# Fifteen of 37 zeroing transfers issued in attention turns 33 to 37, six routing steps a turn from the start, W1's split one half a turn

## The chip, the cores and the metric

The kernel runs on one core of one Trainium2 chip. The metric is device time in microseconds (us): the median of three runs of the kernel before is 985.14 us (985.03 to 985.75). Engines are named as in the profile: PE is TensorE (PEld its weight loads), DVE VectorE, ACT ScalarE, POOL GpSimd. SP issues DMA transfers; "SPq" is its queue of issues.

## The reference: what is computed

Local attention over chunks of 64 positions, then a mixture of 8 experts of which each token takes two.

```python
def _attn_ref(q, k, v):                 # (8, 8, 576, 64) each
    scores = scale * matmul(q_c, k_c^T)         # per chunk of 64
    attn = exp(scores - max); attn /= sum + 1e-9
    return matmul(attn, v_c)
...
def _moe_ref(x, w_gate, w_noise, noise, w1, w2):   # x: (4608, 512)
    noisy_logits = x @ w_gate + log1p(exp(x @ w_noise)) * noise
    top2 = the two largest of 8; top2_w = softmax over them
    for e in range(8):                  # w1[e]: 512x1024, w2[e]: 1024x512
        h = maximum(x[mask] @ w1[e], 0)
        out[mask] += top2_w[mask, k] * (h @ w2[e])
```

## The kernel before, in words

**Attention in turns.** The 4608 tokens are 36 tiles of 128. `attend(it)` is one turn of a software pipeline: it does the scores of tile it+1, the softmax of tile it, the product with V of tile it-2 (`pv`), the transpose of tile it-3 (`x_trans`, `x_copy`) and, every fourth turn, the gate. Turns 0 to 35 run in a loop; 36 and 37 stand between the first transposes of the expert part, and 38 to 40 are called from inside the first expert block. The program sets the order on each engine by hand (`manual_schedule`): an engine's queue holds its instructions in the order in which the Python code emits them. SP loads Q, K and V in pairs of tiles into rings of three.

**Routing.** `route(g)` is a generator that computes, for a group of four tiles (the last group has eight), the two experts of each token and a slot number in a DRAM list (`lii`). It gives control back before each DVE instruction or pair ("a step"), and a turn takes STEPS steps of it, half before and half after the normalisation (`rc`, `xs`). STEPS is 10 up to turn 13 and 6 after it. When a group is routed, its eight scatters go into `pending`.

**Scatters.** `scatter` (L606 to L623) emits on POOL one or two small memsets (L619), a copy that reads an operand of this turn, so that the scatter keeps its place (L621), and an indirect DMA that writes 128 token rows to `slots` in DRAM (L623). There are 72: group 3 is complete with the 32nd, group 6 with the 56th, the last group with the 72nd. The 32nd is followed by SP's loads of the rows of block 0, the 56th by those of block 1, the last by those of block 2 (`gather`, L170); each of these loads waits until the scatters before it have landed.

**Zeroing.** Results are added to `out` by indirect DMA, so all 37 pieces of 128 rows of `out` are first written with zeros (`zero_out`, L691 to L694, 256 KB each, issued by SP). They are emitted after `layer1` of block 0, which puts them on SP's queue behind the row loads of block 1 and ahead of those of block 2.

**W1's split.** The matmuls are float32r in three terms, so each weight is split into a high part (ACT, L88) and a low part (L89). For expert 0's W1 (four chunks `c`, two halves each) the low part is computed on POOL; the eight halves are emitted two a turn in turns 8 to 11.

**Experts.** Each expert has about 1200 rows in three blocks of about 384. `layer1(i)` does 96 matmuls of 384 columns (L236), `layer2(i)` products of 512 columns (L236 too). While `layer2(1)` runs, its hook transposes the rows of block 2 on PE (`x_tile`, L219) at four fixed places; the first is after the sixth step of row tile 0. All of SP's later loads follow in its queue.

Of the kernel before, what the change touches and what calls it, by code (L numbers as in the profile page):

```python
# [49 lines left out]
def kernel(ctx, tc, qT, kT, vh, wgn, noise, w1, w2, out, caps=CAPS):  # L50
    nc = tc.nc
# [15 lines left out]
    def w_load(e, which, c):  # L67
        st = stage.tile([P, 1024], FT, name="st")
        staged[e, which, c] = st
        if which == 1:  # L70
            if e == 0:
                nc.sync.dma_start(st, w1[0, c * P:(c + 1) * P, :])
            else:
                for j in range(4):
                    nc.sync.dma_start(st[32 * j:32 * j + 32], w1v[ds(place[e], 1), c, j].rearrange("o r f -> (o r) f"))
        else:
            nc.sync.dma_start(st.rearrange("p (f n) -> p f n", f=2),
                              w2[ds(place[e], 1) if e else slice(0, 1), 2 * c * P:(2 * c + 2) * P, :]
                              .rearrange("o (f p) n -> p (o f) n", f=2))

    def w_split(e, which, c, half, eng=None):
        if half == 0:
            W[e, which, c] = (wpool[which].tile([P, 1024], FR, name=f"w{which}h{c}"),
                              wpool[which].tile([P, 1024], FR, name=f"w{which}l{c}"))
        hi, lo = W[e, which, c]
        st = staged[e, which, c]
        s = slice(half * 512, half * 512 + 512)
        nc.scalar.activation(hi[:, s], st[:, s], AF.Copy)  # L88
        (eng or nc.vector).tensor_sub(lo[:, s], st[:, s], hi[:, s].bitcast(FT))  # L89
# [243 lines left out]
    def load_qk(j):  # L333
        if j < NT // 2:
            QB[j] = loads.tile([P, 2, 4, P], FT, name="qb", bufs=RING)
            for h in range(2):
                nc.sync.dma_start(QB[j][h::2], qT[HALF[h], 2 * j:2 * j + 2])
                nc.sync.dma_start(KB[j % RING][h::2, h], kT[HALF[h], 2 * j:2 * j + 2])

    def load_v(j):  # L340
        if j < NT // 2:
            for h in range(2):
                nc.sync.dma_start(VB[j % RING][h::2, h], vh[HALF[h], 2 * j:2 * j + 2])
# [76 lines left out]
    def scores(t):  # L420
        for hp in range(4):
            for q in HALF:
                nc.tensor.matmul(PS[q, t % 2, hp * P:(hp + 1) * P], QB[t // 2][:, t % 2, hp, q],  # L423
                                 KB[t // 2 % RING][:, :, t % 2, hp, q], start=True, stop=True)

    def soft_max(t):
        mx = work.tile([P, 4, 2], FT, name="mx", bufs=6)
        nc.vector.tensor_reduce(mx, sco[t % 2], AX.X, OP.max)  # L428
        return mx

    def soft_sub(t, mx):
        PR[t] = work.tile([P, 512], FT, name="pr")
        nc.vector.tensor_tensor(by_head(PR[t]), sco[t % 2], mx[:, :, :, None].to_broadcast([P, 4, 2, 64]), OP.subtract)  # L433

    def soft_exp(t):
        nc.scalar.activation(PR[t], PR[t], AF.Exp, scale=0.125)

    def p_trans(t):
        for hp in range(4):
            nc.tensor.transpose(PS[:, 2, hp * P:(hp + 1) * P], PR[t][:, hp * P:(hp + 1) * P], ident)  # L440

    def p_copy(t):
        PT[t] = work.tile([P, 4, P], FT, name="pts", bufs=2)
        nc.scalar.activation(PT[t].rearrange("p a b -> p (a b)"), PS[:, 2, :], AF.Copy)
# [3 lines left out]
    def pv(t):  # L448
        for hp in range(4):
            for c, q in enumerate(HALF):  # L450
                o = 130 * (hp % 2)
                nc.tensor.matmul(PS[q, 3 + hp // 2, o:o + 130], PT[t][:, hp, q],  # L452
                                 VB[t // 2 % RING][:, :, t % 2, c, hp, :], start=True, stop=True)

    def norm_a(t):
        RC[t] = work.tile([P, 2, 4, 1], FT, name="rc", bufs=6)
        nc.scalar.activation(RC[t], pvb[:, :, :, 64:65], AF.Identity, bias=eps)

    def norm_b(t):
        nc.vector.reciprocal(RC[t], RC[t])  # L460
# [4 lines left out]
    def x_trans(t):  # L465
        x = XS[t // 4][:, t % 4]
        for d in range(ND):
            nc.tensor.transpose(PS[:, 5, d * P:(d + 1) * P], x[:, d * P:(d + 1) * P], ident)  # L468

    def x_copy(t):  # L470
        g, r = divmod(t, 4)
        if r == 0:
            XT[g] = gx.tile([P, ND, 4, P], FT, name="xt", bufs=1)
        nc.scalar.activation(XT[g][:, :, r, :], PS[:, 5, :].rearrange("p (d n) -> p d n", d=ND), AF.Copy)
# [3 lines left out]
    def gate_mm(g):  # L478
        for d in range(ND):
            nc.tensor.matmul(PS[32 * d:32 * d + 32, 6, :], wg[:, d, :], XT[g][:, d], start=True, stop=True)  # L480
# [7 lines left out]
    def gate_turn(g):  # L488
        for r in range(4):
            nc.tensor.transpose(PS[:, 6, r * P:(r + 1) * P], LS[g][:, r, :], ident)  # L490
# [170 lines left out]
    def step_route(phase, most=99):  # L661
        for r in list(routing):
            while r[1] == phase and most > 0:
                if phase == "dve":
                    most -= 1
                r[1] = next(r[0], None)
            if r[1] is None:
                routing.remove(r)

    def next_turn():  # L670
        for r in routing:
            if r[1] == "wait":
                r[1] = next(r[0])
# [13 lines left out]
    wq = list(halves)  # L687
    zeros = list(range(NROWS // P))

    def zero_out(n):  # L690
        for _ in range(n):  # L691
            if zeros:
                r = zeros.pop(0)
                nc.sync.dma_start(out[r * P:(r + 1) * P, :], zero[:, 0:DM])  # L694

    def attend(it):
        STEPS = 6 if it > 13 else 10
        if it % 2:
            load_qk((it - 1) // 2 + 3)
        if it % 2 == 0 and it >= 4:  # L700
            load_v((it - 4) // 2 + 3)
        if it in (9, 11):
            for r in range(CLEAN + 64 * (it // 2 - 4), CLEAN + 64 * (it // 2 - 3), 16):
                nc.sync.dma_start(slots[r * NE:(r + 16) * NE, 0:USED], zero)
        if it == 11:
            nc.sync.dma_start(slots[(CLEAN + P) * NE:NLIST * P * NE, CODE:USED].rearrange("(p r) c -> p r c", p=P),
                              zero[:, 0:3 * (NLIST * P - CLEAN - P) // 16].rearrange("p (r c) -> p r c", c=3))
        if it in range(4, 8):
            w_load(0, 1, it - 4)
        if it in (29, 31, 33, 35):  # L710
            w_load(0, 2, (it - 29) // 2)
        next_turn()
        if it == 0:
            scores(0)
        if it <= 1:
            p_trans(0) if it else scores(1)
        if 0 < it < NT - 1:
            scores(it + 1)
        if 0 <= it - 2 < NT:
            pv(it - 2)  # L720
        gated = it - 4 >= 0 and (it - 4) % 4 == 3
        if gated:
            gate_mm((it - 4) // 4)
        if 0 < it - 1 < NT:
            p_trans(it - 1)
        if 0 <= it - 3 < NT:
            x_trans(it - 3)
        if it - 5 >= 0 and (it - 5) % 4 == 3:
            gate_turn((it - 5) // 4)
            if grp_of[it - 5] != grp_of.get(it - 4):  # L730
                r = route(grp_of[it - 5])
                routing.append([r, next(r)])
        step_route("pe")
        if 0 <= it - 2 < NT:
            norm_a(it - 2)
        if 0 <= it - 1 < NT:
            p_copy(it - 1)
        if it < NT:
            mx = soft_max(it)
            soft_sub(it, mx)  # L740
            scatter(1, mx[0:1, 0, 0:1])
            soft_exp(it)
        if 0 <= it - 3 < NT:
            x_copy(it - 3)
        if gated:
            gate_copy((it - 4) // 4)
        step_route("dve", STEPS // 2)
        if 0 <= it - 2 < NT:
            norm_b(it - 2)
            scatter(1, RC[it - 2][0:1, 0, 0])  # L750
            norm_c(it - 2)
        if it - 5 >= 0 and (it - 5) % 4 == 3:
            gate_sum((it - 5) // 4)
        step_route("act")
        step_route("dve", STEPS // 2)
        if it == NT + 2:
            scatter(2, XT[(it - 3) // 4][0:1, 0, (it - 3) % 4, 0:1])
        elif it == NT + 3:
            scatter(2, LS[(it - 4) // 4][0:1, 0, 0:1])
        if it in range(8, 12):  # L760
            for _ in range(2):
                w_split(0, 1, *wq.pop(0), eng=nc.gpsimd)

    for it in range(NT):
        attend(it)
# [16 lines left out]
    rot["tr"] = 1  # L782
    x_tile(0, 0)
    attend(NT)
    x_tile(0, 1)
    x_tile(0, 2)
# [220 lines left out]
```

## Time and profile before

| | |
|---|---|
| median of three runs | 985.14 us |
| the profiled execution: time, span | 983.39 us, 981.6 us |
| PE, DVE, ACT, POOL busy | 97%, 47%, 29%, 24% |
| turns 0 to 35 (attention) | 0 to about 131 us |
| block 0, block 1, the rest of the experts | from 137 us, from 175 us, from 206 us |
| DMA moved | 132.93 MB, 135 GB/s on average |

A row of a timeline gives start, duration, engine, line, operation and operands, and in brackets how long the engine stood idle before and what ended that. A row of the windows gives, for one stretch, the busy time of each engine with its instruction count, the granted TensorE clock (1.00 is 2.4 GHz, 0.50 is 1.2 GHz) and the busy share of the 16 DMA engines. A stretch whose clock stands between the two held some of each.

### The profile page before, as it was taken

How to read it: one execution, taken by the hardware profiler on the slowest of the kernel's cores; microseconds unless marked ns; L12 is line 12 of the kernel's file. 1: busy time of each engine (PE TensorE's matmuls, PEld its weight loads, DVE VectorE, ACT ScalarE, POOL GpSimd, SP SyncE). 2: the span in 40 equal slices, each digit the busy share in tenths (PEclk: the TensorE clock that was granted, in tenths of full speed). 3: DMA queues.
4: the chain of work that ended last, by engine and by line, in shares of the span. 5: the costliest groups of instructions: out<-in, count | busy, mean ns of one | idle time of the engine just before them, and what ended most of it. 6: DMA issues, size and time to landing. Idle time of an engine off the chain costs nothing.

```text
span 981.6 us, 16116 instructions
## 1 busy us (share of the span) xinstructions
PE 949.9 (97%) x5752; PEld 845.1 (86%) x5752; DVE 459.5 (47%) x1014; ACT 287.8 (29%) x623; POOL 234.8 (24%) x424
## 2 busy tenths in 40 slices
PE   6999999969999999999999999999999999999996
PEld 5778888949897998989898899889998998899885
DVE  6888966214454642554254435443434344434311
ACT  3666662103142421332142213122312231223100
POOL 3366668430201011111101110210111011111112
PEclk9999999979999999999999999999999999999999
DMA  8999965997702643165227522653174216412213
GB/s 303 361 340 374 348 238 213 382 235 137 182 25 48 173 111 44 33 154 140 35 37 149 141 44 33 138 145 54 22 161 129 52 25 161 108 14 30 33 22 44
DMA packets 97155, 132.93 MB, mean 135 GB/s; under 512 B 23440, under 2 KB 56592, under 8 KB 97072
## 3 DMA queue, kind: packets, MB, share of 16 engines
q1 hardware_dynamic: 80160, 92.50, 31.1%
q0 software_dynamic: 16432, 38.33, 19.6%
q8 instruction: 46, 0.75, 0.3%
q10 hardware_dynamic: 480, 1.05, 0.3%
q14 instruction: 37, 0.30, 0.1%
HBM read 81.69 MB, written 50.13 MB: 134 GB/s over the span
## 4 chain that ended last, share of the span: by engine, by line
PE 88%; SPq 4%; DVE 3%; issue 1%; DMA 1%; POOL 1%; ACT 1%; ACTq 0%; DVEq 0%; POOLq 0%
PE PS L236 77%; SPq L694 3%; PE PS L423 3%; PE PS L452 3%; PE PS L440 2%; PE PS L468 1%; PE PS L288 1%; PE PS L480 1%; DVE xs L463 1%; POOL out L203 0%; DMA kb<-in_kT 0%; DMA xg<-slots 0%; DVE mx L428 0%; DVE pr L433 0%; PE PS L490 0%
## 5 line engine op out<-in xcount | busy, mean ns | idle before, releaser
L203 POOL DMA_INDIRECT out<-o,lid x74 | 115.0, 1554 | 646.2 <-DVE o L271 627.0
L236 PE MATMUL PS<-xh,w1h 128*128 128x384 f32 (+2 forms) x768 | 261.3, 340 | 0.0
L236 PE MATMUL PS<-xh,w1l 128*128 128x384 f32 (+2 forms) x768 | 260.5, 339 | 0.0
L236 PE MATMUL PS<-xl,w1h 128*128 128x384 f32 (+2 forms) x768 | 260.4, 339 | 0.0
L255 ACT ACTIVATE hh<-PS 128x384 fp32r<-128x384 f32 (+2 forms) x192 | 95.2, 496 | 463.0 <-PE PS L236 456.9
L236 PE MATMUL PS<-w2h,hh 128*128 128x512 f32 x584 | 228.8, 392 | 0.0
L236 PE MATMUL PS<-w2h,hl 128*128 128x512 f32 x584 | 228.4, 391 | 0.0
L236 PE MATMUL PS<-w2l,hh 128*128 128x512 f32 x584 | 228.3, 391 | 0.0
L258 DVE SCALAR_TENSOR_TENSOR hl<-PS,hh 128x384 fp32r<-128x384 f32 (+2 forms) x192 | 108.7, 566 | 176.1 <-ACT hh L255 144.1
L271 DVE TENSOR_SCALAR o<-PS,lwt 128x512 f32<-128x512 f32 (+2 forms) x74 | 55.4, 749 | 229.5 <-PE PS L236 223.0
L236 PEld LDWEIGHTS PS<-xh,w1h 128*128 128x128 f32 x768 | 144.3, 188 | 5.9 <-issue 4.2
L236 PEld LDWEIGHTS PS<-xl,w1h 128*128 128x128 f32 x768 | 144.3, 188 | 1.6
L236 PEld LDWEIGHTS PS<-xh,w1l 128*128 128x128 f32 x768 | 144.2, 188 | 0.9
L236 PEld LDWEIGHTS PS<-w2h,hl 128*128 128x128 f32 x584 | 109.5, 188 | 23.4
L236 PEld LDWEIGHTS PS<-w2h,hh 128*128 128x128 f32 x584 | 109.7, 188 | 22.6
L236 PEld LDWEIGHTS PS<-w2l,hh 128*128 128x128 f32 x584 | 109.7, 188 | 22.6
L623 POOL DMA_INDIRECT slots<-xs,lii x72 | 71.2, 989 | 26.3 <-issue 23.5
L226 ACT ACTIVATE xh<-y 128x512 fp32r<-128x512 f32 x67 | 41.2, 614 | 92.4 <-DVE y L223 92.4
L227 DVE TENSOR_TENSOR xl<-y,xh 128x512 fp32r<-128x512 f32 x67 | 45.0, 671 | 47.9 <-ACT xh L226 47.9
L423 PE MATMUL PS<-kb,qb 128*64 128x128 f32 x576 | 42.0, 292 | 8.4 <-DMA kb<-in_kT 6.6
L202 POOL MEMSET spacer<- 1x1 f32 x77 | 47.3, 614 | 0.0
L223 DVE STREAM_TRANSPOSE y<-xg 128x512 f32<-128x512 f32 x67 | 45.6, 680 | 0.0
(128 smaller groups left out, 692.3 us busy)
## 6 DMA issues: line engine op xcount, KB each, us to landing
st<-in_w SPq DMA_DIRECT2D x36, 512.0 KB, 6.7
xg<-slots SPq DMA_DIRECT2D x252, 64.0 KB, 2.0
st<-in_w SPq DMA_DIRECT2D x112, 128.0 KB, 4.1
out<-zero SPq DMA_DIRECT2D x37, 256.0 KB, 4.4
vb<-in_vh SPq DMA_DIRECT2D x36, 260.0 KB, 5.2
qb<-in_qT SPq DMA_DIRECT2D x34, 256.0 KB, 5.7
kb<-in_kT SPq DMA_DIRECT2D x32, 256.0 KB, 5.5
xg<-slots SPq DMA_DIRECT2D x9, 256.0 KB, 3.0
```

Of the source, the lines that this page charges most:

```text
L202: nc.gpsimd.memset(spacer, 0.0)
L203: s = nc.gpsimd.indirect_dma_start(out=out, out_offset=bass.IndirectOffsetOnAxis(ap=rows_of(i, j)[0:r], axis=0), in_=o[0:r], in_offset=Non ...
L223: nc.vector.transpose(y[:, 0:4 * r], x[:, 0:4 * r])
L226: nc.scalar.activation(oh, src, AF.Copy)
L227: nc.vector.tensor_sub(ol, src, oh.bitcast(FT))
L236: nc.tensor.matmul(p, a, b, start=first and n == 0, stop=last and n == 2)
L255: nc.scalar.activation(hh[:, 0:n], p, AF.Relu)
L258: nc.vector.scalar_tensor_tensor(hl[:, 0:n], p, 0.0, hh[:, 0:n].bitcast(FT), op0=OP.max, op1=OP.subtract)
L271: nc.vector.tensor_scalar(o[0:r], p[0:r], w, None, op0=OP.mult)
L423: nc.tensor.matmul(PS[q, t % 2, hp * P:(hp + 1) * P], QB[t // 2][:, t % 2, hp, q], KB[t // 2 % RING][:, :, t % 2, hp, q], start=True, stop ...
L452: nc.tensor.matmul(PS[q, 3 + hp // 2, o:o + 130], PT[t][:, hp, q], VB[t // 2 % RING][:, :, t % 2, c, hp, :], start=True, stop=True)
L623: s = nc.gpsimd.indirect_dma_start(out=slots, out_offset=bass.IndirectOffsetOnAxis(ap=lii[:, k, t0 + r:t0 + r + 1], axis=0), in_=XS[(t0 + ...
```

## The change

`STEPS` is 6 in all turns. In each of turns 33 to 37 `zero_out(3)` stands behind the second half of the routing steps, so that 15 of the 37 pieces are emitted there; the call after `layer1` of block 0 stays and emits the 22 that are left. The eight halves of expert 0's W1 are emitted one a turn in turns 7 to 14.

```diff
     def attend(it):
-        STEPS = 6 if it > 13 else 10
+        STEPS = 6
...
         step_route("act")
         step_route("dve", STEPS // 2)
+        if it in range(33, 38):
+            zero_out(3)
...
-        if it in range(8, 12):
-            for _ in range(2):
-                w_split(0, 1, *wq.pop(0), eng=nc.gpsimd)
+        if it in range(7, 15):
+            w_split(0, 1, *wq.pop(0), eng=nc.gpsimd)
```

On SP, from turn 32 on: the last V load (`vb`), the last two loads of W2 (`st`), the rows of block 1 (`xg`, `meta`) and, at the end, those of block 2 (three tiles and one of 64 rows).

```order
 L343 DMA vb_113<-in_vh 64x1040 x2
-L77 DMA st<-in_w 128x2x512 x2
+L77 DMA st<-in_w 128x2x512
+L694 DMA out<-zero 128x512 x6
+L77 DMA st<-in_w 128x2x512
+L694 DMA out<-zero 128x512 x9
 L170 DMA xg<-slots 128x512 x3
 L638 DMA meta_89<-slots 128x3x3
-L694 DMA out<-zero 128x512 x37
+L694 DMA out<-zero 128x512 x22
 L170 DMA xg<-slots 128x512 x3
 L170 DMA xg<-slots 64x512
```

Fifteen zeroing transfers moved ahead of block 1's rows; the V load stands ahead of all of them, one W2 load behind six.

On POOL, before, the low parts of W1 (two halves to a row) and the first scatter, whose copy reads `mx` of turn 13:

```order
L89 TENSOR_TENSOR w1l_529<-st,w1h_528 128x512 x2
L89 TENSOR_TENSOR w1l_597<-st,w1h_596 128x512 x2
L89 TENSOR_TENSOR w1l_649<-st,w1h_648 128x512 x2
L89 TENSOR_TENSOR w1l_715<-st,w1h_714 128x512 x2
L619 MEMSET spacer 1x1 x2
L621 COPY spacer<-mx 1x1
L623 DMA slots<-xs,lii 44032x576
```

The same place now; the first scatter's copy reads `rc` of turn 14:

```order
L89 TENSOR_TENSOR w1l_478<-st,w1h_477 128x512 x2
L89 TENSOR_TENSOR w1l_589<-st,w1h_588 128x512 x2
L89 TENSOR_TENSOR w1l_702<-st,w1h_701 128x512 x2
L89 TENSOR_TENSOR w1l_815<-st,w1h_814 128x512
L619 MEMSET spacer 1x1 x2
L621 COPY spacer<-rc 1x1
L623 DMA slots<-xs,lii 44032x576
L89 TENSOR_TENSOR w1l_815<-st,w1h_814 128x512
L619 MEMSET spacer 1x1 x2
L621 COPY spacer<-mx 1x1
L623 DMA slots<-xs,lii 44032x576
```

The first scatter stands three places of the turns later (turn 14's second instead of turn 13's first), and one half of W1 stands behind it.

On DVE, before, turn 9 and the start of turn 10, from the first routing step of group 0 on:

```order
L521 SCALAR_TENSOR_TENSOR gu<-gu,gy 128x32
L523 TENSOR_TENSOR gsp<-gsp,gu 128x32
L525 SCALAR_TENSOR_TENSOR gsp<-lg,gsp 128x32
L527 TENSOR_TENSOR gsp<-gsp,nz 128x32
L529 TENSOR_TENSOR gsp<-gsp,lg 128x32
L460 RECIPROCAL rc<-rc 128x8
L463 TENSOR_TENSOR xs<-PS,rc 128x512
L535 MAX gm<-gsp 128x8 x4
L539 MAX_INDEX gmi<-gm,gsp 128x8 x4
L543 TENSOR_TENSOR goh<-e_row,gmi 128x32
L428 TENSOR_REDUCE mx<-PS 128x8
```

The same place now:

```order
L521 SCALAR_TENSOR_TENSOR gu<-gu,gy 128x32
L523 TENSOR_TENSOR gsp<-gsp,gu 128x32
L525 SCALAR_TENSOR_TENSOR gsp<-lg,gsp 128x32
L460 RECIPROCAL rc<-rc 128x8
L463 TENSOR_TENSOR xs<-PS,rc 128x512
L527 TENSOR_TENSOR gsp<-gsp,nz 128x32
L529 TENSOR_TENSOR gsp<-gsp,lg 128x32
L535 MAX gm<-gsp 128x8 x2
L428 TENSOR_REDUCE mx<-PS 128x8
```

Two instructions fewer stand ahead of `rc` and `xs`, and the maxima and indices spread into the next turn.

## Rows read from the trace of the kernel before

**Rows 1.** The page: the chain that ended last, shares by engine

```profile
PE 88%; SPq 4%; DVE 3%; issue 1%; DMA 1%; POOL 1%; ACT 1%; ACTq 0%; DVEq 0%; POOLq 0%
```

**Rows 2.** PE's waits, first 225 us: total us, times, longest

```profile
PE PS L219 <- DMA xg<-slots: 9.5, 1, 9.5
```

**Rows 3.** The chain that ended last, 155 to 215 us: start, us, what

```profile
160.96 2.75 DMA slots<-xs,lii
...
191.67 0.65 SPq L694
...
201.93 4.27 DMA xg<-slots
206.25 1.12 PE PS L219 x4
207.37 4.03 PE PS L236 x12
211.83 2.76 PE PS L236 x12
```

**Rows 4.** Timeline of SP's issues, 123 to 202 us

```profile
123.90 1.21 SPq L343 DMA_DIRECT2D vb<-in_vh  x2
...
163.73 1.34 SPq L170 DMA_DIRECT2D xg<-slots  x3
...
165.73 36.09 SPq L694 DMA_DIRECT2D out<-zero  x37
```

**Rows 5.** The first 22 zeroing issues (L694): duration ns min/median/max, start us

```profile
L694 SPq DMA_DIRECT2D out<-zero x22: 481/1252/1667, 165.7 to 191.1; - x22
```

**Rows 6.** Row loads of block 2 (L170, 200 to 206 us): issue to landing

```profile
DMA to landing us min/median/max: 4.4/4.4/4.4
```

**Rows 7.** Timeline of PE: two places of it

```profile
131.48 1.11 PE L452 MATMUL PS<-vb,pts 128*64 128x130 f32 x16
...
167.56 0.60 PE L219 MATMUL PS<-ident,xg 128*128 128x128 f32 x4
```

**Rows 8.** Windows of all engines; the first row names the columns

```profile
core 0: us, PE busy (x) PEld busy (x) DVE busy (x) ACT busy (x) POOL busy (x), PEclk, DMA share, GB/s
35.30:64.57 29.27, 25.42 (x311) 20.61 (x310) 25.27 (x85) 18.85 (x46) 16.01 (x27) 0.94 0.98 338
67.94:91.26 23.32, 23.31 (x307) 19.16 (x306) 20.31 (x78) 14.79 (x38) 16.07 (x49) 1.00 0.99 367
42.50:46.00 3.50, 3.06 (x24) 2.66 (x24) 3.34 (x10) 2.49 (x6) 0.38 (x2) 0.53 1.04 378
...
137.00:157.00 20.00, 19.29 (x128) 17.89 (x126) 14.16 (x74) 9.87 (x23) 15.08 (x34) 1.00 0.39 150
...
200.00:204.00 4.00, 0.00 (x0) 0.00 (x0) 0.00 (x0) 0.00 (x0) 0.00 (x0) 0.50 1.01 352
```

**Rows 9.** Scatters (L623), 155 to 185 us: duration ns, start us; issue to landing

```profile
L623 POOL DMA_INDIRECT slots<-xs,lii x21: 956/982/998, 154.4 to 183.0; - x21
...
DMA to landing us min/median/max: 2.7/6.4/8.0
```

**Rows 10.** The V load of 123.9 us (L343): issue to landing

```profile
DMA to landing us min/median/max: 6.1/6.1/6.1
```

**Rows 11.** Timeline of POOL: a pair of halves, scatters 1, 2 and 32

```profile
37.65 2.50 POOL L89 TENSOR_TENSOR w1l<-st,w1h 128x512 fp32r<-128x512 f32 x2 [28.60 <-ACT w1h L88]
...
56.75 1.18 POOL L623 DMA_INDIRECT slots<-xs,lii  x1 [1.49 <-DMA kb<-in_kT]
...
58.88 1.00 POOL L623 DMA_INDIRECT slots<-xs,lii  x1 [0.47 <-issue]
...
117.81 0.98 POOL L623 DMA_INDIRECT slots<-xs,lii  x1 [0.44 <-issue]
```

**Rows 12.** Timeline of DVE: the same product in group 0 and in group 1

```profile
37.76 1.21 DVE L527 TENSOR_TENSOR gsp<-gsp,nz 128x32 f32<-128x32 f32 x1
...
56.25 0.19 DVE L527 TENSOR_TENSOR gsp<-gsp,nz 128x32 f32<-128x32 f32 x1
```

## The prediction, made before the changed kernel ran

> **What bounds the kernel now.** I read the chain that ended last first: PE carries 88% of it and SP's queue 4% [rows 1]. The rest is read where the chain leaves PE. Of PE's waits in the first 225 us one stands out: 9.5 us of the transposes of L219 for a row load [rows 2]. The chain in order of time says why [rows 3]: the 56th scatter (160.96 us) lets SP load block 1's rows at 163.73, then SP issues 37 zeroing transfers in 36.09 us [rows 4], and only behind them, at 201.93, stand block 2's rows. They land 4.3 us later, and PE, idle since 206.25 - 9.5 = 196.75, goes on at 206.25. It goes on slowly: in the idle stretch the granted clock had fallen to 0.50, the lower level of 1.2 GHz [rows 8], and the four transposes take 1.12 us where the same four took 0.60 at full clock [rows 7], twelve matmuls 4.03 us where the next twelve take 2.76 [rows 3]. The stall thus costs 9.5 + 0.52 + 1.27 = 11.3 us. Behind it PE runs without gaps for most of 750 us, so that what is saved here reaches the end.
>
> A second place is the start of routing. Turns 9 to 15 take 29.27 us and turns 17 to 23, with as many gate turns, 23.32 [rows 8]: 5.95 us more, part of it waits, part a stretch at 0.53 of the clock.
>
> **Part 1: 22 instead of 37 transfers ahead of block 2's rows.** The first 22 start between 165.7 and 191.1 us [rows 5], and the next stands at 191.67 [rows 3]. Block 2's rows are then issued at 191.67 instead of 201.93, 10.26 us earlier. With the 4.4 us that they took to land behind a full queue of the same transfers [rows 6] they are there at 196.07. PE wants them at 196.75: a margin of 0.68 us. The wait goes, the clock does not fall, the sum is -11.3 us. What is late next is near: the last of the 72 scatters, which these loads wait for, and whose kind takes 6.4 us to land in this stretch, 8.0 at most [rows 9]. It is issued at 183.0 [rows 9], so it lands between 189.4 and 191, just ahead of the issue. Bounds of this part: -11.3, and, with a remaining wait of 4 us (below), -5.5.
>
> **Part 2: fifteen transfers in turns 33 to 37.** In the order they stand on SP behind the last V load (123.90 us) and ahead of block 1's rows, which SP cannot issue before 163.73 [rows 4]. Between these SP has some 37 us in which it only waits. Fifteen issues at 0.98 us (36.09 / 37) to 1.25 us [rows 5] are 15 to 19 us, and end near 145. One load of W2 stands behind six of them, so about 7 us later; its halves are split in the last quarter of block 0's first layer, after 150 us. The data are 15 x 256 KB = 3.9 MB, at the 378 GB/s of the windows when the engines are full [rows 8] 10.4 us of all DMA engines. From 137 to 157 us these are busy 0.39 of the time [rows 8], which leaves 12 us. So I cost this part at nothing; its cover is that idle DMA time, and without it it is the slow rival below.
>
> **Part 3: six steps and one half a turn.** In turns 8 to 11 ACT and POOL now split one half, not two, and DVE takes two instructions fewer ahead of `rc` and `xs` in turn 9. The turns from 9 on can gain between 0 and 5.95 us. I expect most of it at that place, and almost none of it at the end, because scatters set the pace: POOL issues them one behind the other, the second at 58.88 and the 32nd at 117.81 [rows 11]. The 32nd releases SP, whose V load for the last two tiles is issued at 123.90 and 124.5 and lands 6.1 us later [rows 4, 10], at 130.6. PE takes that V at 131.48 [rows 7]. PE can thus come at most 0.9 us earlier here, however early the turns before it are, unless the scatters are earlier too.
>
> Are they? The first started at 56.75 after waiting 1.49 us for a DMA, not for its turn [rows 11]. In the changed order it stands three places later, in turn 14, but turn 14 comes earlier by what the turns gain, so I take it at the same time. Behind it POOL now has one half of W1, 2.50 / 2 = 1.25 us [rows 11]. The chain of scatters is later by 1.25 us at the most, and earlier by 0.25 if the 1.49 us go; later turn waits inside the chain shrink when turns are early. I take +0.7.
>
> PE then waits before that V product, for up to 5.95 - 0.9 = 5 us, and the clock may fall. The trace has two prices for it: about 3.5 x 0.47 = 1.6 us in the stretch from 42.5 to 46 us, after a short wait [rows 8], 1.8 after the long one. Since PE is not the bound of turns 36 to 38 I take half, 0.9. Part 3: -0.9 + 0.7 + 0.9 = +0.7 us, between -1.2 and +2.2. It moves block 1's rows and PE alike, so part 1 keeps its margin.
>
> The shared-port rule of the Trainium skill ("SBUF — State Buffer", "SBUF: two separate sides") speaks against this part: a DVE operation with two SBUF inputs and a GpSimd operation that reads SBUF lock each other out for a whole instruction. The same DVE product takes 1.21 us while POOL splits W1 and 0.19 when it does not [rows 12], which agrees. What it would cost is a rival.
>
> **Sum.** -11.3 + 0.7 = -10.6 us. The profiled execution took 983.39 us with a span of 981.6, the median is 985.14, 1.75 above; against its own time the changed kernel should take 972.8 in a profile and, by the median, 974.5 us.
>
> **Rivals.**
>
> Block 2's rows are still late (20%). If all 22 issues keep the median of 1.25 us, they end at 165.73 + 22 x 1.25 = 193.2; if SP then also waits for the last scatter, or the rows need the 6 to 8 us that scatters took, they land at 198 to 201, and PE waits 2 to 4 us, with up to 1.8 us of clock. The gain is 10.6 minus 2 to 5.8, the time 976.5 to 980.3. For it speaks that the margin is 0.68 us; against it that the first 22 did end at 191.67 in this trace.
>
> The low halves on POOL hold DVE up (10%). Each of eight halves in its own turn could hold DVE for 1.21 - 0.19 = 1.0 us; in the trace pairs of halves do this in four turns. Eight such holds, of which the turns before had some four, are 4 us more. If they delay the first scatter, everything behind it is later by that: 978.5. Against it: a product that comes after the half has ended pays nothing.
>
> The early turns' gain arrives (8%). Were the V load no limit, because the scatters start 3 to 5 us earlier, the end would gain as much more: 970 to 971.5. Against it: the 1.49 us wait on a DMA at the first scatter, and the half behind it.
>
> The zeroing comes out of the scatters' time (9%). If the moved 10.4 us of DMA work are not hidden in 126 to 157 us but delay the 56th scatter by all of that, block 1's rows are issued at 174 instead of 163.73. PE wants them at 167.56 [rows 7], 3.8 us after that issue, about what a landing takes, so it waits 10 us and restarts at the low clock, 1.8 us; and 22 issues at 1.25 us from 176 on end at 203.5, block 2's rows land at 208, when PE, 11.8 us late, wants them. The end is later by 11.8 - 11.3 = 0.5 us and, if those rows too take 6 to 8 us, by 2 to 4: about 988. It decides from about 9 us of delay. Against it: beside 22 zeroing transfers scatters land in 2.7 to 8.0 us [rows 9], which is 5 us from best to worst, and not 10.
>
> The Trainium skill speaks to this in "DMA: Bandwidth & Descriptors", "Queues, rings and completion order": each DMA engine takes turns between the queues that have work; by it zeroing would halve the scatters' rate while it lasts. The spread of landings agrees. It is over before the 56th by the sum of part 2.
>
> **How the numbers follow.** The forecast has 53% (972.5 to 976.5 alone). With the late rows, the held DVE and part of the early gain the range is 971.0 to 980.0 us. About 2 us (0.2%) is what a measurement of this kernel can tell from no change. Faster: 53 + 20 + 10 + 8 = 91%, less a little for cases that add up: 90%. The slow rival is split: 5% same, 5% slower.
>
> **What would show it.** In the profile after, PE's wait of L219 for the row load under 1 us and no stretch at 0.50 near 200 us (part 1); SP's 15 issues between 125 and 147 us, block 1's rows issued within 2 us of 163.7 (part 2); turns 9 to 15 within 23 to 27 us, and then a new wait of PE for V (L452) of 2 to 5 us near 127 us (part 3). The prediction is wrong if PE waits over 2 us at block 1's or block 2's transposes, or if the V wait is absent and block 0 starts over 3 us earlier.

## The result, and the profile after

The changed kernel takes 971.59 us (median; 970.72 to 972.59), the kernel before beside it 985.24 (985.03 to 985.75): a ratio of 0.9861 [0.9844, 0.9878], 13.65 us faster. The forecast was 974.5 us, its range 971.0 to 980.0. The profiled execution takes 970.72 us where that of before takes 983.39, 12.67 us less; its span is 968.9 us.

The chain of the page, where [rows 1] had SP's queue with 4%, has none of it; most of what it follows is PE:

```profile
PE 84%; issue 1%; POOL 0%; DVE 0%; ACT 0%; POOLq 0%
```

PE's waits in the first 215 us (total us, times, longest), where [rows 2] had the wait for a row load:

```profile
PE PS L236 <- DVE hl L258: 1.4, 1, 1.4
PE PS L452 <- ACT ls L484: 1.4, 1, 1.4
```

No wait of L219 for `xg` is among them. SP's issues in the same stretch answer to [rows 4]: start, duration, line, operands.

```profile
120.36 1.33 SPq L170 DMA_DIRECT2D xg<-slots  x3
...
122.48 2.20 SPq L343 DMA_DIRECT2D vb<-in_vh  x2
...
125.36 5.44 SPq L694 DMA_DIRECT2D out<-zero  x6
130.90 1.11 SPq L77 DMA_DIRECT2D st<-in_w  x1
132.05 10.82 SPq L694 DMA_DIRECT2D out<-zero  x9
161.38 1.31 SPq L170 DMA_DIRECT2D xg<-slots  x3
...
163.36 26.03 SPq L694 DMA_DIRECT2D out<-zero  x22
189.63 2.20 SPq L170 DMA_DIRECT2D xg<-slots  x4
```

Fifteen transfers are out by 142.9 us, block 1's rows follow at 161.38, and block 2's stand at 189.63 instead of 201.93. The chain in order of time, where [rows 3] had the late load and what it cost:

```profile
165.03 0.44 PE PS L219 x4
...
180.26 15.50 PE PS L236 x81
195.76 0.44 PE PS L219 x4
196.20 2.77 PE PS L236 x12
```

The transposes of block 2 run at 195.76 without a wait, and the twelve matmuls behind them take 2.77 us, not 4.03. Windows of all engines, columns as in [rows 8]:

```profile
35.26:59.46 24.20, 23.52 (x306) 19.16 (x306) 21.15 (x74) 18.07 (x45) 10.84 (x15) 1.00 1.02 363
...
125.00:137.00 12.00, 10.64 (x108) 8.85 (x104) 8.24 (x39) 6.17 (x14) 8.73 (x24) 1.00 1.01 360
137.00:157.00 20.00, 19.25 (x118) 17.24 (x117) 14.50 (x72) 9.18 (x21) 16.88 (x40) 1.00 0.85 325
190.00:200.00 10.00, 10.00 (x51) 8.38 (x50) 3.18 (x13) 1.64 (x3) 5.70 (x7) 1.00 0.85 190
```

Turns 9 to 15 (first row) take 24.20 us at full clock, 5.1 less than before; the moved zeroing raises the DMA share of 137 to 157 us from 0.39 to 0.85; around 195 us the clock is 1.00.

The account of the profiled 12.67 us: block 1's first transposes start at 164.87 on the timeline, not at 167.56 [rows 7], which is 2.7 us; the stall of 9.5 us and its low clock (0.52 + 1.27) are gone, 11.3 us; a new wait of 1.4 us at 180.26 takes some back. 2.7 + 11.3 - 1.4 = 12.6.

### The profile page after: what moved, and what is told of

It is laid out like the page before. It is cut to its first block, busy times and chain, and to the rows that moved or that the text cites. A ratio compares the mean times of both kernels' runs of the same rounds, so it can differ in the third digit from the quotient of the medians.

```text
span 968.9 us, 16115 instructions
## 1 busy us (share of the span) xinstructions
PE 946.4 (98%) x5752; PEld 841.6 (87%) x5752; DVE 457.9 (47%) x1014; ACT 287.3 (30%) x623; POOL 234.8 (24%) x424
## 4 chain that ended last, share of the span: by engine, by line
PE 84%; issue 1%; POOL 0%; DVE 0%; ACT 0%; POOLq 0%
PE PS L236 82%; PE PS L288 1%; POOL out L203 0%; PE PS L219 0%; PE PS L452 0%; PE PS L468 0%; PE PS L490 0%; PE PS L480 0%; DVE o L271 0%; PE PS L440 0%; DVE hl L258 0%; ACT hh L255 0%; ACT ls L484 0%; PE PS L558 0%; PE PS L556 0%
## 5 line engine op out<-in xcount | busy, mean ns | idle before, releaser
L623 POOL DMA_INDIRECT slots<-xs,lii x72 | 71.3, 990 | 25.2 <-issue 22.7
```

The costliest lines, as they stand in the source:

```text
L623: s = nc.gpsimd.indirect_dma_start(out=slots, out_offset=bass.IndirectOffsetOnAxis(ap=lii[:, k, t0 + r:t0 + r + 1], axis=0), in_=XS[(t0 + ...
```

## The experiments

Executions differ by up to 3.7 us before turn 9 begins (last section), so beside the times stands a table of the profiles, one execution of each kernel, in us from turn 9's V product (from the timeline's starts): turn 36's V product, block 1's and block 2's first transposes, and the end (profiled time less the start of turn 9's product).

| kernel | turn 9 at | turn 36 | block 1 | block 2 | end |
|---|---|---|---|---|---|
| before | 36.23 | 95.25 | 131.33 | 170.02 | 947.16 |
| after | 36.18 | 93.13 | 128.69 | 159.42 | 934.54 |
| e10, after once more | 36.25 | 93.18 | 129.02 | 158.08 | 932.96 |
| e1, zeroing only | 37.59 | 96.58 | 132.72 | 163.37 | 938.81 |
| e2, turns only | 36.39 | 93.35 | 128.79 | 168.42 | 945.12 |
| e3, ten steps | 36.75 | 98.16 | 134.23 | 164.86 | 940.09 |
| e4, W1 in pairs | 37.13 | 91.83 | 131.08 | 167.79 | 942.68 |
| e5, 10 moved | 37.32 | 93.25 | 128.81 | 160.97 | 936.06 |
| e6, 25 moved | 37.99 | 93.84 | 129.86 | 159.87 | 934.90 |
| e7, V load ahead | 39.91 | 91.02 | 128.05 | 160.78 | 935.80 |
| e8, copy between | 37.84 | 92.87 | 129.88 | 158.91 | 933.80 |
| e9, twelve in run | 36.63 | 93.89 | 131.97 | 161.00 | 936.00 |
| e11, one memset | 37.34 | 90.03 | 126.10 | 155.13 | 930.18 |

The same changed kernel had ratios of 0.9861 and 0.9874 in two comparisons, so differences of about 1 us between kernels of different comparisons tell nothing.

### The two parts by themselves

e1 is the kernel before with part 2's calls alone:

```diff
+        if it in range(33, 38):
+            zero_out(3)
```

> Only the fifteen zeroing transfers are moved; the turns are as before. Theory (the stall at block 2's rows was 9.5 us and 1.8 us of low clock, the early turns give the rest): 11.3 us less than before, 973.9 us, PE's wait of L219 under 1 us, no stretch at clock 0.50 near 200 us, block 1's rows issued at 163.7 us as before. Rival (the zeroing alone gives everything, the early turns nothing at the end): 971.6 us. Second rival (the moved transfers delay the 56th scatter and only the earlier turns hid that): block 1's rows issued after 165 us and a time above 976 us.

975.05 us, ratio 0.9894 [0.9879, 0.9908], 10.65 less than the 985.70 beside it. No wait of L219 and no half clock near 200 us remain. That is the theory's case. Its profile (976.40 us) does show what the second rival took for its sign, block 1's rows issued after 165 us (166.48). But from turn 9's product that is only 1.4 us later than before. Of these 1.0 are there at turn 34's product (127.61), before the first moved transfer leaves SP (127.70), and 0.3 more at turn 35's, so that most of it is not the zeroing's.

e2 is the changed kernel without these calls (all 37 behind block 1's rows):

> Only the turns are changed (six steps throughout, one half of W1 a turn in turns 7 to 14); all 37 zeroing transfers stay behind block 1's rows. Theory (the early turns gain 5 us where they are and about 2.4 at the end, because the 32nd scatter holds turns 34 to 36): 982.9 us, PE's wait of L219 still 8 to 10 us, block 1's rows issued near 161.4 us. Rival (the early turns' 5 us arrive whole): 980 us. Second rival (nothing of it arrives, because the 37 transfers start no earlier): 985 us and block 1's rows at 163.7 us.

981.51 us, ratio 0.9962 [0.9949, 0.9974], 4.2 less. That is between its theory (2.4 less than before) and its rival (all 5 us arrive). The stall is back, and there is a new wait for V:

```profile
PE PS L219 <- DMA xg<-slots: 8.4, 1, 8.4
PE PS L452 <- DMA vb<-in_vh: 1.5, 1, 1.5
```

In e2's profile turns 9 to 15 take 24.21 us, as in the changed kernel: 5.1 us less than before, of which 2 to 4.2 arrive. The two parts sum to 14.8 us by medians (10.4 by the table's last column) where both together gave 13.65 and 12.9 (12.6 and 14.2): additive within some 1 to 4 us, by which executions differ also behind turn 9; more is not shown. e2 also prices the moved transfers by themselves: without them block 1's rows are issued 125.50 us after turn 9's product, with them 125.20 (after) and 125.97 (e10).

### The two halves of part 3

e3 takes the step count back, e4 the split of W1.

```diff
-        STEPS = 6
+        STEPS = 6 if it > 13 else 10
```

> The changed kernel with ten steps a turn up to turn 13 as before; halves of W1 one a turn, zeroing moved. Theory (both edits of the turns matter: pairs of halves hold ACT, ten steps hold DVE ahead of rc and xs): turns 9 to 15 about 26.5 us, between the 24.2 of the change and the 29.3 of before, but the end only 0.5 to 1.5 us above the change, 972.1 to 973.1 us. Rival (the steps alone decide the early turns): turns 9 to 15 near 29 us and about 974 us. Second rival (the first scatter, a turn and a half earlier again, starts the chain earlier and the end gains): below 971 us.

```diff
-        if it in range(7, 15):
-            w_split(0, 1, *wq.pop(0), eng=nc.gpsimd)
+        if it in range(8, 12):
+            for _ in range(2):
+                w_split(0, 1, *wq.pop(0), eng=nc.gpsimd)
```

> The changed kernel with W1's halves two a turn in turns 8 to 11 as before; six steps throughout, zeroing moved. Theory (both edits matter): turns 9 to 15 about 26.5 us, the second scatter 1.3 us earlier relative to the first because no half stands between them, the end within 1.5 us of the change: 971 to 973 us. Rival (the pairs alone decide the early turns): turns 9 to 15 near 29 us and about 974 us. A DVE operation with two SBUF inputs that meets a half should take up to 1.25 us in this kernel, as L527 did before.

e3 took 977.07 us (ratio 0.9916 [0.9902, 0.9930]), e4 975.84 (0.9897 [0.9874, 0.9921]; three of its runs at 972.6 to 973.7, three at 978.0 to 979.8, so that the median lies where no run does, and the profile is of the latter). Windows of turns 9 to 15, first of e3:

```profile
35.82:66.51 30.69, 25.72 (x311) 20.19 (x310) 26.64 (x86) 18.40 (x45) 15.10 (x27) 0.94 0.92 328
...
60.00:62.00 2.00, 0.16 (x2) 0.19 (x4) 1.90 (x5) 0.34 (x1) 1.43 (x5) 0.92 0.78 300
62.00:64.00 2.00, 2.00 (x20) 1.63 (x23) 0.98 (x2) 0.12 (x1) 1.43 (x5) 0.50 0.53 208
```

and of e4:

```profile
36.20:61.44 25.24, 23.89 (x306) 19.17 (x305) 22.18 (x73) 18.50 (x46) 12.47 (x16) 1.00 1.00 360
```

Ten steps take 28.9 us with pairs (e1) and 30.7 with single halves, six steps 25.2 with pairs and 24.2 with single halves. So the steps are the larger lever (3.7 to 6.5 us in these turns). The split gains 1.0 us there with six steps; with ten it costs 1.8, and by medians 2.0 at the end (e3 against e1). In e3 PE is busy for 0.16 of 2 us before its clock stands at 0.50. The expectation for e3, that it loses about a microsecond, was wrong: turn 36 comes 5 us later, without a wait for V, and the end 5.5.

At the end the split's gain with six steps is not seen. e4's turn 36 comes at 91.83, 1.3 us earlier than in the changed kernel and without a wait, though its V load left SP at the same place (86.26 us after turn 9's product, 86.30 in the changed kernel): its V was there more than 1 us sooner, whether by the pairs or by chance is not shown. The time of e4's profile is lost behind it, in waits of 1.70 us near 150 and of 4.62 us near 180 us (below), each with a low clock; its three short runs are 12.0 to 13.1 us under the 985.70 beside them, as the changed kernel is (13.65 and 12.9).

### How much zeroing to move

```diff
-            zero_out(3)
+            zero_out(2)   # e5; zero_out(5) in e6
```

> The changed kernel with two zeroing transfers a turn instead of three: 10 moved, 27 left ahead of block 2's rows. Theory (the stall of block 2's rows grows with the zeroing left ahead of them): 22 transfers took 26.0 us in the profile after and block 2's rows had landed before PE wanted them, so five more issues at 0.98 to 1.19 us put these rows 4.9 to 6 us later, near 195. PE, which asked at about 195.3, then waits 3 to 5 us and runs a stretch at half clock (1 to 1.8 us): 975.5 to 978.5 us. Rival (any zeroing moved is enough, the stall hung on the queue being full): no wait of L219, 971 to 973 us. Rival (the zeroing left is slower when more of it stands there): wait over 6 us, 980 us or more.

> The changed kernel with five zeroing transfers a turn: 25 moved, 12 left ahead of block 2's rows. Theory (the zeroing moved lies in DMA time that is free, and with 22 left the stall is gone already, so that more moved brings nothing): 971 to 973 us, no wait of L219, block 2's rows issued as soon as the last scatters have landed, about 189 to 190 us. Slow rival (zeroing comes out of the scatters' time): ten more transfers of 256 KB at the 378 to 400 GB/s of full engines are 6.5 to 7 us of all DMA engines; if they delay the 56th scatter, block 1's rows are issued near 168 instead of 161.4 and PE waits at L219 for them by 2 to 4 us: 974 to 977 us. Rival (fewer transfers beside the last scatters make these and block 2's rows earlier and shorten the late ACT and DVE work near 179 us): 969.5 to 971 us.

e5 took 973.10 us (ratio 0.9874 [0.9857, 0.9891]), e6 972.89 (0.9870 [0.9852, 0.9888]). In e5 the wait of L219 is back, at once and small (timeline of PE):

```profile
198.29 0.66 PE L219 MATMUL PS<-ident,xg 128*128 128x128 f32 x4 [1.16 <-DMA xg<-slots]
```

SP issues block 2's rows in the three kernels, with 27, 22 and 12 transfers ahead, at (timelines of e5 and e6):

```profile
164.73 29.53 SPq L694 DMA_DIRECT2D out<-zero  x27
194.38 2.33 SPq L170 DMA_DIRECT2D xg<-slots  x4
```

```profile
166.60 13.54 SPq L694 DMA_DIRECT2D out<-zero  x12
188.76 1.99 SPq L170 DMA_DIRECT2D xg<-slots  x4
```

From turn 9 that is 157.06 (e5), 153.45 (after) and 150.77 (e6). In e5 the 27 transfers take 3.5 us longer than the 22 (29.53 and 26.03), and PE goes on 3.9 us after the issue of the rows, 1.16 us late. With 3.9 us the rows of the changed kernel are there at 157.4, where PE asked at 159.4; but 1.4 us of this margin are the pause at 180 us (below), and in e10, which has no pause, the rows are there at 154.06 + 3.9 = 158.0 and PE asks at 158.08. So 22 are just enough. e5's wait is smaller than the 3 to 5 us of its theory because its execution has such a pause too, of 1.5 us: 1.16 + 1.5 = 2.7. No half clock followed. In e6 SP stands idle from 180.1 to 188.8, so that there the last scatters set the issue, and not the zeroing; it brings nothing. The slow rival of e6 did not show: block 1's rows were issued 0.7 to 1.5 us later from turn 9 than in the changed kernel (126.69), not 6.6, and PE waited 0.24 us for them.

### What caps the early turns

e7 puts the last V load ahead of block 0's rows on SP:

```diff
-        if it % 2 == 0 and it >= 4:
+        if it % 2 == 0 and it >= 4 and it != 32:
...
+        if it == 31:
+            load_v(17)
```

> The changed kernel with the last V load emitted in turn 31 behind that turn's product, ahead of block 0's row load on SP, so that it no longer waits for the 32nd scatter. Theory (the V load behind the 32nd scatter sets when turn 36's product starts, and nothing else is right behind it): the V load leaves SP 2 us or more before 120.4 us, the V product runs 1.2 to 1.4 us earlier than at 129.31, and 0.5 to 1.4 us arrive at the end: 970.2 to 971.1 us. Rival (the next limit is at the same place: the scatters and block 0's rows, which come 2.2 us later on SP for the V load ahead of them): the V wait turns into a wait of L219 for block 0's rows or of the copies of turn 36, and the time stays within 971 to 973 us.

971.86 us, ratio 0.9865 [0.9847, 0.9884]. Turn 36's product comes 2.1 us earlier from turn 9 (91.02), without a wait; at block 1 0.6 to 1.0 is left (against after and e10), and PE waits there 0.54 us for its rows, which the 56th scatter releases. So the cap is real, and the next one stands behind it, at block 1's rows and not, as the rival had it, at block 0's. At the end nothing of it is seen: in this profile ACT's pause (below) costs PE 1.8 us and some 4 us at a clock of 0.50 to 0.69, and the median is about that of the changed kernel.

Both caps hang on scatters. e11 makes POOL's work for each shorter in the turns:

```diff
-            for _ in range(2 if attending[0] else 1):
+            for _ in range(1):
                 nc.gpsimd.memset(spacer, 0.0)
```

> The changed kernel with one small memset instead of two ahead of each scatter of the attention turns. POOL stands behind its scatters without a gap there: their period is 1.90 us with two memsets and 1.47 us with one. Theory (POOL's own period sets when the 32nd scatter lands, that sets the V load behind it, and that sets turn 36's product, so that what the turns gain is waited away there): the 32nd scatter comes up to 30 x 0.43 = 13 us earlier, bounded by when its group is routed; block 0's rows and the V load leave SP well before 118 us, PE's wait of 1.4 to 3.4 us at turn 36's product goes, and so do 1.5 to 3.5 us at the end: 968 to 970 us. Rival (the routing, not POOL's period, is the limit): the scatters wait for the list of slots (lii) instead, block 0's rows are issued within 2 us of 120.4 us and the time stays within 970 to 973 us. Slow rival (scatters that come earlier stand beside the Q, K and V loads, which then are late): PE waits for kb or vb in turns 16 to 34 by 2 us or more: 973 to 977 us.

967.40 us, ratio 0.9822 [0.9808, 0.9835]: by the medians 3.4 to 4.2 us faster than the changed kernel, and the best version here. POOL's timeline in the changed kernel, a scatter and the next:

```profile
60.10 1.02 POOL L623 DMA_INDIRECT slots<-xs,lii  x1 [0.47 <-issue]
61.13 0.23 POOL L619 MEMSET spacer<- 1x1 f32 x2
61.42 0.18 POOL L621 COPY spacer<-rc 1x1 f32<-1x1 f32 x1
62.05 0.98 POOL L623 DMA_INDIRECT slots<-xs,lii  x1 [0.44 <-issue]
```

and in e11:

```profile
66.73 0.98 POOL L623 DMA_INDIRECT slots<-xs,lii  x1 [0.16 <-DVE rc L460]
67.71 0.09 POOL L619 MEMSET spacer<- 1x1 f32 x1
67.86 0.18 POOL L621 COPY spacer<-rc 1x1 f32<-1x1 f32 x1
68.19 0.99 POOL L623 DMA_INDIRECT slots<-xs,lii  x1 [0.16 <-issue]
...
72.62 0.18 POOL L621 COPY spacer<-rc 1x1 f32<-1x1 f32 x1 [1.89 <-DVE rc L460]
```

In the changed kernel the period is 1.95 us here and 1.90 in nearly all of the first 32: POOL sets it. In e11 it is 1.47, until at 72.62 POOL has caught up with the turns and its copy waits for DVE's `rc`; from there on the turns set the pace, two scatters to a turn, mostly 1.47 to 1.97 us apart. The 32nd scatter comes 74.9 us after turn 9's product instead of 81.4, block 0's rows 80.1 instead of 84.2, turn 36's product 90.03 instead of 93.13, and against e10 it keeps 2.9 us at block 1, 3.0 at block 2 and 2.8 at the end. The slow rival (loads that come late for it) did not show. What the turns gain (5.1 us) is now there at block 1: 131.33 less 126.10 is 5.2.

### The new wait at 180 us

e10 is the changed kernel once more.

> The changed kernel once more, unchanged, beside the two that follow. Both theories: 971 to 973 us where turn 9 starts at 36.2 us. If the start-up alone differs between executions (turn 9's V product came at 36.2 to 39.9 us in the profiles so far, with a K load as the last thing waited for), some of its runs come 1 to 4 us later with nothing else changed.

It took 970.75 us beside 983.68, ratio 0.9874 [0.9858, 0.9891], with runs from 969.21 to 972.94. ACT's timeline in the first profile:

```profile
170.54 0.60 ACT L226 ACTIVATE xh<-PS 128x512 fp32r<-128x512 f32 x1 [1.92 <-PE PS L219]
179.12 1.25 ACT L255 ACTIVATE hh<-PS 128x384 fp32r<-128x384 f32 x3 [7.98 <-PE PS L236]
```

and in this one:

```profile
171.01 0.60 ACT L226 ACTIVATE xh<-PS 128x512 fp32r<-128x512 f32 x1 [1.93 <-PE PS L219]
175.17 0.49 ACT L255 ACTIVATE hh<-PS 128x384 fp32r<-128x384 f32 x1 [3.56 <-PE PS L236]
```

In one ACT took block 1's first hidden tile when its matmuls were done; in the other the matmuls of three tiles were done before it took the first, 4 us later. The profiles of after and of e1 to e7 all show such a pause of ACT, 6.5 to 8.4 us, which ends 1.8 to 2.2 us after POOL's run of nine scatters without a copy; in e4 it held an `xh` and cost PE 4.62 us, and some 6 us more ran at half clock:

```profile
PE PS L236 <- ACT xh L226: 4.6, 1, 4.6
```

Before, e8, e9, e10 and e11 do not show it. Two kernels were to tell whether that run holds ACT:

```diff
             if f % 3 == 0:
-                scatter(1)
+                scatter(1, e_row[0:1, 0:1])   # e8
```

> The changed kernel with a one-element copy of a constant ahead of each of the nine scatters in block 0's second layer, as the other scatters have one; their period should go from 1.26 to 1.47 us and the run of nine should end 1.9 us later, near 179.1 us. In eight of nine profiles ACT, idle for 6.5 to 8.3 us, went on 1.9 to 2.2 us after the last scatter of this run. Theory (ACT and DVE are held while POOL issues scatters back to back, until the run ends): ACT's first hh of block 1 comes at about 181.0 instead of 179.1, PE's wait there grows from 1.4 to about 3.3 us, and the time is 973 to 975.5 us. Rival (it is the missing copy that holds them): the wait goes, 970 to 971 us. Rival (the two are unrelated): the wait stays at 1.0 to 1.8 us, 971 to 973 us.

```diff
-            if f % 3 == 0:
+            if f % 2 == 0:   # e9
                 scatter(1)
```

> The changed kernel with twelve instead of nine scatters in block 0's second layer (every second step instead of every third), so that the run back to back is three longer and the three behind block 1's first hidden tile go. Theory (ACT is held until the run ends): the run ends 3 x 1.26 = 3.8 us later, near 181.0, ACT's first hh of block 1 comes near 183, PE waits 5 us or more there and runs a stretch at half clock (1.5 us): 976 to 978.5 us. Rival (unrelated): ACT's hh stays at 179 and the last scatter is 3 us earlier, so that block 2's rows have more margin: 971 to 973 us.

e8: 972.09 us, ratio 0.9887 [0.9871, 0.9904]; e9: 970.77, ratio 0.9862 [0.9846, 0.9879]. In e9 the run lasts until 184.43, and ACT works through it (178.46, on time):

```profile
178.46 0.49 ACT L255 ACTIVATE hh<-PS 128x384 fp32r<-128x384 f32 x1 [3.59 <-PE PS L236]
```

So a run of scatters does not by itself hold ACT: it did not in e9, nor in e10 with the run of nine. What holds ACT in the executions that have the pause, and why it ends where the run does, is not tested, since neither e8 nor e9 had it; and that e8 has none says nothing for its copy. The pause is not fixed by the kernel, as after and e10 are the same. It may go with the chip: e1 to e7 ran on two chips and e8 to e11 on a third, and those of before and after are not on record. Its cause stays open.

These profiles do show something on part 3's clock. Turn 36's wait is 2.98 us in e10, with full clock behind it; in e8 it is 2.62 and in e9 3.40 us, and in both the clock falls. Windows of e8 (one row) and of e9:

```profile
133.00:135.00 2.00, 2.00 (x11) 2.00 (x10) 0.60 (x2) 1.09 (x2) 1.43 (x5) 0.50 1.04 408
```

```profile
129.00:131.00 2.00, 0.48 (x5) 0.51 (x7) 1.01 (x5) 0.00 (x0) 1.35 (x5) 0.58 0.89 297
...
133.00:135.00 2.00, 2.00 (x11) 2.00 (x10) 0.80 (x2) 1.14 (x2) 1.33 (x4) 0.50 1.02 404
```

and of e10 at the same place:

```profile
126.00:129.00 3.00, 0.45 (x5) 0.21 (x2) 1.11 (x6) 2.25 (x5) 1.94 (x8) 1.00 0.98 323
...
131.00:133.00 2.00, 2.00 (x22) 1.83 (x21) 1.25 (x3) 1.61 (x4) 1.43 (x5) 1.00 1.04 406
```

e9's block 1 is 3 us later than e10's for it (131.97 and 129.02).

## Why the prediction was right, point by point

**Part 1 held, in mechanism and size.** Forecast -11.3 us; e1, which has parts 1 and 2 alone, gave 10.65. The 22 issues took 26.03 us, 0.09 more than from 165.73 to 191.67 before. Block 2's rows came earlier than forecast (189.63, not 191.67) because block 1's did, and so did PE's demand (195.6, not 196.75), which the 1.4 us of ACT's pause made later still. The margin, 0.68 us in the text, was 2 us with the pause and next to nothing without it (e10): rightly called small. The rival of late rows did not show at 22 and begins at 27: e5 waits 1.16 us. It did not carry the 1 to 1.8 us of low clock that the rival added.

**Part 2 held: cost 0.** Fifteen issues from 125.36 to 142.9, forecast 125 to 147, and block 1's rows at 161.38, not later than the 163.73 of before; that is 2.3 us from it, just outside the 2 us that were to show this part, and early, by part 3. e2, without the moved transfers, issues these rows no earlier (125.50 us from turn 9's product, against 125.20 and 125.97). The added DMA share, 0.46 of 20 us between 137 and 157, is 9.2 us of the 10.4 worked out. Ten more transfers (e6) cost nothing either. The slow rival had no part in it.

**Part 3 was mis-sized, and the end is earlier for it.** The term stood at +0.7 us, between -1.2 and +2.2, and measured -2.7 at block 1. By its pieces: turns 9 to 15 took 24.20 us (23 to 27 forecast). The wait before turn 36's V product came, 1.4 us here and 3.0 in e10 where 2 to 5 were forecast. The profile names ACT's `ls` for it here and DVE's `gex` in e10; in e2, e6 and e9 it is for V, and e7, which only loads that V earlier, has no wait. So the cap was rightly named. But it stood earlier than worked out:

- The cap, -0.9, taken from the V product's start less the landing of V, and the scatters, +0.7, were to give -0.2 together. Turn 36's product came at 129.31, not 131.48: -2.2. The V load left SP at 122.48, 1.4 us earlier than the 123.90 of before, so the 0.9 held, and the scatters' term was -1.4 in place of +0.7. This is the step that failed.
- Two things made it so. The second scatter came at 60.10 (60.13 by the half of W1 behind the first), but the 32nd at 117.60, 0.2 us ahead of the 117.81 of before [rows 11]: the chain made up its late start, because turns that come early leave POOL fewer waits (beyond 30 periods of 1.90 us, 0.5 us now and 1.9 before). The prediction names this effect and gives it little, 1.25 down to 0.7. And block 0's rows, ahead of V on SP, were loaded at 120.36, 2.8 us after the 32nd scatter, where before it was 4.2 (121.98); scatters took 2.9 to 4.2 us to land there before, and the one landing that e10's trace shows 2.8. Why they land sooner is not shown.
- The clock, +0.9. It did not fall in the profile after or in e10, and fell in e8 and e9. A half of a price that is paid whole or not at all was a fair mean, and not what one profile shows.

Behind turn 36 another 0.5 us were gained up to block 1. The rival "the early turns' gain arrives" thus held in part: 2.7 of 5.1 us. It needed the cap to move, and the text put the cap where one execution had it. 971.59 us lies only 0.6 us above the lower end of the range, and below 972.5 to 976.5, the band of the forecast by itself: the range held because its lower end had room for this rival, which was given 8%.

**The halves on POOL held DVE little.** The trace of the changed kernel has one routing operation of 1.00 us in these turns, where [rows 12] had 1.21 and others like it:

```profile
54.11 1.00 DVE L521 SCALAR_TENSOR_TENSOR gu<-gu,gy 128x32 f32<-128x32 f32 x1
```

That rival fell: a product that does not meet a half pays nothing. The shared-port rule of the Trainium skill ("SBUF — State Buffer", "SBUF: two separate sides") agrees with this operation too: it ends at 55.11 us, and the half that POOL splits beside it, 53.80 and 1.28 us long, at 55.08. e3's theory, that single halves gain part of the early turns also with ten steps (26.5 us), fell too: they took 30.7, against 28.9 with pairs.

**In sum**, -10.6 was forecast; the profile has -11.3 for part 1, -2.7 for part 3 and +1.4 for ACT's pause, -12.6, and the medians -13.65 and, in e10, -12.9. The step that failed is the +0.7 of part 3, within it the scatters' term. That the forecast missed the profile by 2 us and not by 3.4 is luck: ACT's pause, which nobody had foreseen, took 1.4 back.

## What to carry to other kernels

Where a queue issues in order and waits most of the time, put bulk transfers that nobody waits for into its idle stretch, and count which wait then ends last: here 22 left were enough, 27 were not, and 12 gained nothing more. A faster stage gains only up to the next thing that paces it; look at the engine that issues without a gap (here POOL, 1.90 us a scatter), and shorten its period before speeding up what runs beside it. Build a cap from the chain of starts that sets it, and not from the clock time at which one execution had it.

## What was not expected of the hardware

- The second memset of one element ahead of a scatter costs more than the 0.14 us that it is busy (0.23 for two, 0.09 for one): where nothing else held POOL, the period fell from 1.90 to 1.47 us without it. Once the turns set the pace less was gained; the 32nd scatter came 6.5 us earlier, 0.2 us a scatter.
- Turn 9's V product came at 36.2 to 39.9 us although the kernels hold the same instructions up to turn 7. In e7 a K load made PE wait 2.48 us ahead of turn 5's V product, and the clock fell behind it (0.93 from 20 to 25 us, 0.72 from 25 to 30).
- Much the same wait of PE at turn 36 was followed by half clock in two executions (2.62 and 3.40 us, e8 and e9) and by full clock in another (2.98 us, e10).
- ACT pauses near 180 us in eight of thirteen profiles, with work at hand and nothing that the profile shows to hold it.
